# W2 by whole rows, and batch 0's second product in two rounds of twelve row blocks

## The chip, the cores and the metric

The kernel runs on one core of a Trainium2 chip. The metric is the device time of one execution in microseconds (us). The engines are TensorE (PE in the profile; its weight loads are PEld), VectorE (DVE), ScalarE (ACT), GpSimd (POOL) and SyncE (SP). SP only issues DMAs here; POOL computes and issues DMAs.

## The reference

Attention with normalised queries and keys, then a layer norm and a two-layer MLP with a residual; B, H, S, D = 8, 12, 448, 64, model width 768, hidden width 3072, all in float32:

```
q_n, k_n = rmsnorm(q, g_q), rmsnorm(k, g_k)
attn = softmax(q_n @ k_n.T / 8)            # per batch and head
x  = heads of (attn @ v) side by side      # (8, 448, 768)
xn = (x - mean) / sqrt(var + 1e-6) * g_ln
out = x + relu(xn @ w_ch1) @ w_ch2         # w_ch1 768x3072, w_ch2 3072x768
```

## The kernel before

Matmuls take float16 and sum in float32 in PSUM. A batch's 448 tokens are three tiles of 128 (t = 0, 1, 2) and 64 left over; the left tokens of two batches make one more tile. Heads go in pairs, 48 in all. For each pair seven steps of scores (L405, L411) are followed by the exponential on ACT (L421) and the product with the values (L458, L460), whose sums oA and oB DVE divides and moves into x and xl (`evac_o`, L473 to L480). There is one bank pair for oA and oB, so PE's next product with the values waits for that evacuation.

The order of the work on every engine is the order in which the program is written out. `run_rest` (L976) writes batch b's MLP chunk by chunk and after each chunk as many steps of batch b+1's attention as a quota allows; the quota is such that attention has reached its goal eleven chunks before the end of batch 0's MLP (`TAIL`). From there `run_rest` writes one item of batch 1's layer norm after each chunk (statistics, normalised rows xn, their transposes by SP's DMA, the root), and from the tenth last chunk on one weight sum after each (L763: sums and differences of blocks of W2, which later batches use in their second product).

Batch 0's MLP is `first_mlp`. `up` (L713) makes the hidden layer h, 24 blocks of 128. `down` (L723) is the second product: for each column half g of W2 (384 columns) and each token tile t, 24 matmuls, one for each block of 128 rows of W2, are summed in one PSUM bank; a chunk is six of them (s counts threes of row blocks, a chunk is two values of s). After the last row block, `add` (L754, DVE) multiplies the sum by the token's scale and adds it to x. The banks psC of these sums and psH of the hidden layer come from one pool of three banks (`ps_m`, tag "mlp"), used in rotation: a new sum takes the bank of the third last and waits for what reads that one. Stores of finished tiles are noted in `late` and issued on SP's queue by `store_late` at s = 3 of the next tile; SP's queue also holds the loads of q and k and the transposes (L306 to L318, L688).

W2 lies in on-chip memory as 24 row blocks of 768 columns in float16, and is loaded by `load_w2` on POOL's queue, with conversion from float32. Its first call comes at step 47 of attention and its second at step 71 (`W2_AT`); the second is preceded by a small copy (L613) that makes POOL wait for a DMA transpose of keys. The first call takes the left 384 columns of all 24 row blocks in one DMA, the second the right 384 columns in two DMAs of twelve row blocks.

The chunks of `down` before:

```
for g in range(2):
    for t in range(3):
        for s in range(4):   # a chunk: s = 2s, 2s + 1
```

Of the kernel before, what the change touches and what calls it, by code (L numbers as in the profile page):

```python
# [8 lines left out]
FP32 = mybir.dt.float32  # L9
# [7 lines left out]
ts = bass.ts  # L17
# [3 lines left out]
NDC, NFF = DM // 128, FF // 128  # L21
# [44 lines left out]
HALF, HCOL = NFF // 2, DM // 2  # L66
# [25 lines left out]
class _Fast:  # L92
# [518 lines left out]
    def load_w2(self, g):  # L611
        if g:
            self.nc.gpsimd.tensor_copy(out=self.rr[:, DMA_UNIT:DMA_UNIT + 1],  # L613
                                       in_=self.kU[DMA_UNIT % 2][:, 0:1])
        for c in (slice(0, HALF), slice(HALF, NFF)) if g else (slice(0, NFF),):
            self.nc.gpsimd.dma_start(
                out=self.sh.w2[:, c, ts(g, 384)],
                in_=self.w2[128 * c.start:128 * c.stop, ts(g, 384)].rearrange("(c p) d -> p c d", p=128))

    def tok_tiles(self, b):  # L620
        x = self.xs[b]
# [86 lines left out]
    def first_mlp(self):  # L708

        nc, sh = self.nc, self.sh  # L710
        tiles, xnT, hT, cur = self.tok_tiles(0), self.xnT, self.hS, {}

        def up(f, i):  # L713
            if i == 0:
                cur["h"] = self.ps_m.tile([128, 512], FP32, tag="mlp", name="psH")
            ps = cur["h"]
            for dc in range(3 * i, 3 * i + 3):
                nc.tensor.matmul(ps[:, 0:384], sh.w1[:, dc, ts(f, 128)], xnT[:, dc],
                                 start=(dc == 0), stop=(dc == NDC - 1))
            if i:  # L720
                nc.scalar.activation(out=hT[:, f], in_=ps[:, 0:384], func=AFT.Relu)

        def down(t, g, s):  # L723
            if s == 0:
                cur["ps"] = self.ps_m.tile([128, 512], FP32, tag="mlp", name="psC")
            ps = cur["ps"][:, 0:HCOL]
            for f in range(3 * s, 3 * s + 3):
                nc.tensor.matmul(ps, hT[:, f, ts(t, 128)], sh.w2[:, f, ts(g, HCOL)],
                                 start=(f == 0), stop=(f == NFF - 1))
            if s == 7:  # L730
                self.add(0, t, g, ps)
                if g and t < 2:
                    self.late.append((0, t, slice(0, DM)))
                elif t == 2 and not g:
                    self.late.append((0, t, slice(0, HCOL)))
                elif t == 2:
                    self.store(0, t, slice(HCOL, DM))
            elif s == 3:
                self.store_late()

        for f in range(UP_FIRST, NFF):
            yield 6 * 384 / 2.4, [lambda f=f, i=i: up(f, i) for i in range(2)]
        for g in range(2):
            for t in range(3):
                for s in range(4):
                    yield 6 * HCOL / 2.4, [lambda t=t, g=g, s=s: down(t, g, s)
                                           for s in (2 * s, 2 * s + 1)]

    def store_late(self):
        for a in self.late:  # L750
# [500 lines left out]
```

## Time and profile before

| what | value |
|---|---|
| median of 3 runs | 582.73 us (582.29, 582.73, 582.96) |
| profiled execution | 579.58 us |
| its span | 578.0 us |
| PE busy | 559.5 us (97%) |
| DVE busy | 381.7 us (66%) |
| ACT busy | 364.4 us (63%) |
| POOL busy | 207.0 us (36%) |
| batch 0's second product on PE | 88.3 to 118.4 us |

Start times are microseconds from the start of the span. A row of the timeline has the start, the duration, the engine, the line, the operation with its output and inputs, the shapes and the count; consecutive like instructions are merged, and what the engine waited for stands in brackets. A duration runs to the end of the write, so the next instruction of an engine can start a little before it. PE's matmuls overlap, so the time of many is read from the start of the first to the start of what follows. "w" in a row stands for W1 and W2 both, "w2s" for the memory of the weight sums, "hS" for the hidden layer.

### The profile page before, as it was taken

What the parts mean: (1) busy time and instruction counts of PE and PEld (TensorE: products, weight loads), DVE (VectorE), ACT (ScalarE), POOL (GpSimd) and SP (SyncE); (2) the same over time, 40 slices, a digit from 0 to 9 for tenths busy, and PEclk for the clock granted to TensorE, in tenths of its full rate; (3) what the DMA queues carried; (4) which work ended last, traced back from release to release, by engine and by line L of the source; (5) the groups of instructions that cost most, each with busy time, mean ns of one, the idle gap of its engine ahead of it and who ended that gap; (6) DMA issues with size and microseconds to landing.
All of it is one profiled execution on the core that took longest, in us unless ns stands there. A gap on an engine that the chain in (4) does not pass through costs nothing.

```text
span 578.0 us, 13670 instructions
## 1 busy us (share of the span) xinstructions
PE 559.5 (97%) x5446; PEld 411.9 (71%) x5446; DVE 381.7 (66%) x826; ACT 364.4 (63%) x674; POOL 207.0 (36%) x224
## 2 busy tenths in 40 slices
PE   5788999999999999999999999999999999999997
PEld 4556666687686867777677768777777777878684
DVE  6989567699657586845667586854756743664424
ACT  5998787447675779557775588637777477323130
POOL 5885636404440620654241521644242320020000
PEclk9999999999999999999999999999999999999999
DMA  8999999958672876969663798958743390030201
GB/s 206 251 238 222 214 207 165 193 147 137 124 131 77 158 127 145 127 148 121 121 106 48 184 134 136 128 143 122 145 64 65 119 113 1 1 110 1 83 2 58
DMA packets 178329, 72.59 MB, mean 126 GB/s; under 512 B 138212, under 2 KB 173220, under 8 KB 178260
## 3 DMA queue, kind: packets, MB, share of 16 engines
q1 hardware_dynamic: 133876, 52.52, 44.1%
q0 software_dynamic: 43440, 18.52, 25.2%
q8 instruction: 44, 0.72, 0.5%
q10 hardware_dynamic: 944, 0.62, 0.4%
q14 instruction: 25, 0.20, 0.1%
HBM read 52.76 MB, written 11.01 MB: 110 GB/s over the span
## 4 chain that ended last, share of the span: by engine, by line
PE 77%; DVE 1%; issue 0%; DVEq 0%
PE psH L798 33%; PE psP L821 30%; PE psS L405 7%; PE oA L458 4%; PE oB L460 1%; PE psS L411 1%; DVE qn L83 0%; DVE w2s L763 0%; DVE ssq L265 0%; DVE w L763 0%; DVE xn L662 0%; DVE hS L804 0%; DVE x L475 0%; DVE xl L757 0%; DVE xl L480 0%
## 5 line engine op out<-in xcount | busy, mean ns | idle before, releaser
L421 ACT ACTIVATE E<-psS,rr_all 128x448 f16<-128x448 f32 x336 | 204.6, 634 | 47.3 <-PE psS L405 40.3
L798 PE MATMUL psH<-xnT,w 128*128 128x256 f16 (+1 forms) x2016 | 225.7, 261 | 0.0
L798 PEld LDWEIGHTS <-w 128*128 128x128 f16 x2016 | 172.8, 98 | 24.3 <-issue 4.9
L801 ACT ACTIVATE hS<-psH 128x512 f16<-128x512 f32 x150 | 89.8, 599 | 97.2 <-PE psH L798 93.0
L821 PEld LDWEIGHTS <-hS 128*128 128x128 f16 x1080 | 100.0, 98 | 57.3 <-issue 1.1
L821 PE MATMUL psP<-w,hS 128*128 128x384 f16 x672 | 127.0, 326 | 0.0
L405 PE MATMUL psS<-qU,kU 128*128 128x448 f16 x288 | 100.9, 352 | 5.0 <-ACT E L421 3.2
L458 PEld LDWEIGHTS <-E 128*128 128x128 f16 x1008 | 70.3, 98 | 35.8 <-issue 2.8
L279 POOL TENSOR_TENSOR k<-k,gprod 128x896 f32<-128x896 f32 x18 | 38.9, 2160 | 139.5 <-ACT khl L259 113.2
L804 DVE TENSOR_TENSOR hS<-hS 128x512 f16<-128x512 f16 (+1 forms) x119 | 60.2, 512 | 19.3 <-ACT hS L801 17.8
L821 PE MATMUL psP<-w2s,hS 128*128 128x384 f16 (+1 forms) x408 | 69.9, 321 | 0.0
L458 PE MATMUL oA<-v,E 128*128 128x65 f16 x864 | 66.9, 193 | 1.1 <-ACT E L421 0.6
L757 DVE SCALAR_TENSOR_TENSOR x<-psP,rs_all,x 128x384 f32<-128x384 f32 x60 | 36.4, 617 | 42.4 <-PE psP L821 41.8
L460 PE MATMUL oB<-v,E 128*128 128x65 f16 x288 | 52.0, 193 | 0.1
L832 POOL TENSOR_TENSOR x<-x,hS 128x384 f32<-128x384 f32 x21 | 23.4, 1126 | 76.1 <-ACT hS L900 75.5
L473 DVE RECIPROCAL rec_all<-oA 128x6 f32<-128x6 f32 x48 | 9.2, 193 | 53.6 <-PE oA L458 53.5
L216 POOL DMA_DIRECT2D v<-in_v_dram x54 | 41.5, 781 | 4.0 <-PE oB L460 2.7
L405 PEld LDWEIGHTS <-kU 128*128 128x128 f16 x288 | 28.0, 98 | 11.1 <-issue 2.2
L900 ACT ACTIVATE hS<-hS,rs_all 128x384 f32<-128x384 f32 x27 | 14.6, 604 | 33.0 <-DVE hS L804 33.0
L460 PEld LDWEIGHTS <-E 128*128 128x128 f16 x336 | 32.4, 96 | 0.4 <-DVE xl L480 0.3
L83 DVE SCALAR_TENSOR_TENSOR qn<-q,rr_all 128x256 f16<-128x256 f32 (+2 forms) x69 | 24.8, 420 | 7.2 <-ACT rr_all L269 7.1
L265 DVE TENSOR_REDUCE ssq<-khl 128x14 f32<-128x896 f32 (+1 forms) x24 | 25.5, 1061 | 5.0 <-ACT khl L259 4.8
(145 smaller groups left out, 616.6 us busy)
## 6 DMA issues: line engine op xcount, KB each, us to landing
k<-in_k_dram SPq DMA_DIRECT2D x19, 384.0 KB, 4.2
q<-in_q_dram SPq DMA_DIRECT2D x18, 384.0 KB, 3.9
out_dram<-x SPq DMA_DIRECT2D x14, 384.0 KB, 3.0
w<-in_moe_w_ch_dram POOLq DMA_DIRECT2D x3, 1536.0 KB, 14.3
v<-in_v_dram POOLq DMA_DIRECT2D x54, 64.0 KB, 4.4
out_dram<-x POOLq DMA_DIRECT2D x9, 384.0 KB, 2.7
w<-in_moe_w_ch_dram POOLq DMA_DIRECT2D x1, 2304.0 KB, 22.5
w<-in_moe_w_ch_dram POOLq DMA_DIRECT2D x2, 1152.0 KB, 14.4
```

The costliest lines, as they stand in the source:

```text
L216: nc.gpsimd.dma_start(out[:, :, j, 0:D], main[:, :, j])
L265: nc.vector.tensor_reduce(out=c["ssq"][:, n], in_=c["sq", n], axis=AX.X, op=ALU.add)
L279: (nc.vector if u in DVE_KG else nc.gpsimd).tensor_tensor(out=c["t"][1], in0=c["t"][1], in1=sh.gprod.unsqueeze(1).broadcast_to([128, g, D] ...
L405: nc.tensor.matmul(ps[0][:, 0:S], c["main"][:, ts(i, 128)], c["q"][:, ts(h, S)], start=True, stop=True)
L421: nc.scalar.activation(out=o, in_=x[:, 0:S], func=AFT.Exp, scale=self.units[u][3][:, g:g + 1], bias=EXP_BIAS)
L458: nc.tensor.matmul(oA[:, t, cs], E[:, ts(t, 128)], rhs, start=(i == 0 and t == 0), stop=(i == 6 and t == 2))
L460: nc.tensor.matmul(oB[:, cs], E[:, 320:448], rhs, start=(i == 0), stop=(i == 6))
L757: self.nc.vector.scalar_tensor_tensor(out=x, in0=ps, scalar=self.rs[:, b, t:t + 1], in1=x, op0=ALU.mult, op1=ALU.add)
L798: nc.tensor.matmul(ps[:, i], sh.w1[:, dc, ts(f + i, 128)], self.xnT[:, dc, 256 - N:256], start=(i == 0 and dc == 0), stop=(i == k - 1 and ...
L801: nc.scalar.activation(out=hT[:, f:f + k], in_=ps, func=AFT.Relu)
L804: nc.vector.tensor_tensor(out=out, in0=a, in1=c, op=op)
L821: nc.tensor.matmul(bank[x][:, c], a[:, f], w[:, f, c], start=(start and f == 0), stop=(stop and f == HALF - 1))
```

## The change

`load_w2` loads whole rows of 768 columns: the first call row blocks 0 to 5 and 6 to 11, the second 12 to 17 and 18 to 23, two DMAs each. The product is made in two rounds of twelve row blocks, each summed in a bank of its own and added to x. In the first round (row blocks 0 to 11) the six sums follow each other, two chunks each. In the second round the left half goes a quarter at a time: row blocks 12 to 17 for t = 0, 1, 2 into three banks, then 18 to 23 for t = 0, 1, 2 with an add after each; then come the three right sums, two chunks each. `store_late` is called at s = 5 in place of s = 3. Nothing else is changed; the number of chunks and of matmuls is the same.

```
-        for c in (slice(0, HALF), slice(HALF, NFF)) if g else (slice(0, NFF),):
+        for c in (0, 6) if not g else (12, 18):
             self.nc.gpsimd.dma_start(
-                out=self.sh.w2[:, c, ts(g, 384)],
-                in_=self.w2[128 * c.start:128 * c.stop, ts(g, 384)].rearrange("(c p) d -> p c d", p=128))
+                out=self.sh.w2[:, c:c + 6],
+                in_=self.w2[128 * c:128 * c + 768].rearrange("(c p) d -> p c d", p=128))
...
         def down(t, g, s):
-            if s == 0:
-                cur["ps"] = self.ps_m.tile([128, 512], FP32, tag="mlp", name="psC")
-            ps = cur["ps"][:, 0:HCOL]
+            if s in (0, 4):
+                cur[t] = self.ps_m.tile([128, 512], FP32, tag="mlp", name="psC")
+            ps = cur[t][:, 0:HCOL]
             for f in range(3 * s, 3 * s + 3):
                 nc.tensor.matmul(ps, hT[:, f, ts(t, 128)], sh.w2[:, f, ts(g, HCOL)],
-                                 start=(f == 0), stop=(f == NFF - 1))
+                                 start=(f % HALF == 0), stop=(f % HALF == HALF - 1))
+            if s in (3, 7):
+                self.add(0, t, g, ps)
             if s == 7:
-                self.add(0, t, g, ps)
                 if g and t < 2:
                     self.late.append((0, t, slice(0, DM)))
...
-            elif s == 3:
+            elif s == 5:
                 self.store_late()
...
-        for g in range(2):
-            for t in range(3):
-                for s in range(4):
-                    yield 6 * HCOL / 2.4, [lambda t=t, g=g, s=s: down(t, g, s)
-                                           for s in (2 * s, 2 * s + 1)]
+        for g, s, t in ([(g, s, t) for g in range(2) for t in range(3) for s in range(2)]
+                        + [(0, s, t) for s in (2, 3) for t in range(3)]
+                        + [(1, s, t) for t in range(3) for s in (2, 3)]):
+            yield 6 * HCOL / 2.4, [lambda t=t, g=g, s=s: down(t, g, s)
+                                   for s in (2 * s, 2 * s + 1)]
```

## The prediction

> **What bounds the kernel now.** I read the busy time by stage first, then the instructions in order of time around batch 0's second product, on TensorE (PE) and on VectorE (DVE), then the waits, the DMA landings and the SP queue.
>
> Busy time by stretch (us from the span's start; busy us of each engine with its instruction count; granted clock; DMA share; GB/s):
>
> ```profile
> core 0: us, PE busy (x) PEld busy (x) DVE busy (x) ACT busy (x) POOL busy (x), PEclk, DMA share, GB/s
> 61.00:88.30 27.30, 26.55 (x244) 17.09 (x241) 15.51 (x31) 22.42 (x47) 14.93 (x17) 1.00 1.21 198
> 88.30:107.60 19.30, 19.30 (x180) 12.06 (x178) 11.97 (x26) 14.07 (x24) 8.76 (x10) 1.00 1.26 186
> 107.60:118.40 10.80, 10.80 (x69) 6.51 (x68) 10.61 (x25) 1.82 (x5) 5.54 (x7) 1.00 1.45 187
> 118.40:140.00 21.60, 21.55 (x214) 16.93 (x213) 20.88 (x35) 14.83 (x28) 6.59 (x7) 1.00 0.66 130
> 140.00:540.00 400.00, 400.00 (x3905) 299.07 (x3904) 255.18 (x578) 254.70 (x466) 130.42 (x141) 1.00 0.63 107
> ```
>
> PE is the bound: it has 0.75 us idle from 61 to 88.3, none to 118.4, 0.05 to 140 and none to 540. So the change has at most 0.8 us to win in the stage that it touches, and whatever it makes PE wait there stays in the span, because no later PE wait can shrink. The row to look at twice is that of 107.60 to 118.40: DVE is busy for 10.61 of 10.80 us, and to 140 for 20.88 of 21.60. In these 30 us DVE runs as full as PE, though its share of the span is 66%.
>
> The second product of batch 0 has 144 matmuls, 24 chunks of 6. Their end on PE:
>
> ```profile
> L728 PE MATMUL psC<-w,hS x144: 324/326/336, 88.3 to 118.2; 128*128 128x384 f16 x144
> ...
> 105.03 1.14 PE L728 MATMUL psC<-w,hS 128*128 128x384 f16 x6
> ...
> 107.62 10.90 PE L728 MATMUL psC<-w,hS 128*128 128x384 f16 x66
> 118.36 1.47 PE L798 MATMUL psH<-xnT,w 128*128 128x256 f16 x12
> ```
>
> The reader is to see that the last 66 matmuls, chunks 14 to 24, run without any attention between them (attention has reached its goal), from 107.62 to 118.36: 0.976 us a chunk. So chunk 16 ends at 110.55 and chunk 18 at 107.62 + 5 x 0.976 = 112.50.
>
> DVE in the same stretch:
>
> ```profile
> 101.07 0.62 DVE L757 SCALAR_TENSOR_TENSOR x<-psC,rs_all,x 128x384 f32<-128x384 f32 x1
> 105.72 0.62 DVE L757 SCALAR_TENSOR_TENSOR x<-psC,rs_all,x 128x384 f32<-128x384 f32 x1 [4.04 <-PE psC L728]
> 106.62 1.09 DVE L265 TENSOR_REDUCE ssq<-khl 128x14 f32<-128x896 f32 x1 [0.28 <-ACT khl L259]
> ...
> 112.30 1.01 DVE L662 SCALAR_TENSOR_TENSOR xn<-x,stat,gln 128x768 f16<-128x768 f32 x1
> 113.35 0.62 DVE L757 SCALAR_TENSOR_TENSOR x<-psC,rs_all,x 128x384 f32<-128x384 f32 x1
> 113.88 0.75 DVE L763 TENSOR_TENSOR w2s<-w,w2s 128x1152 f16<-128x1152 f16 x1
> ...
> 116.68 0.61 DVE L757 SCALAR_TENSOR_TENSOR x<-psC,rs_all,x 128x384 f32<-128x384 f32 x1
> ...
> 119.34 0.61 DVE L757 SCALAR_TENSOR_TENSOR x<-psC,rs_all,x 128x384 f32<-128x384 f32 x1
> 119.86 0.75 DVE L763 TENSOR_TENSOR w<-w 128x1152 f16<-128x1152 f16 x1
> ```
>
> The six adds of L757 follow chunks 4, 8, 12, 16, 20 and 24. That of chunk 12 waits 4.04 us for PE: until then DVE has time. From 106.62 it has none: statistics and the normalised rows of batch 1, weight sums and adds run end to end, and the add of chunk 16, whose matmuls end at 110.55, starts at 113.35 and is done at 113.97. DVE is about 2.8 us behind PE. Today nobody minds, because the bank that it frees is wanted a whole bank rotation later.
>
> **The change, part by part.** *The load of W2.* The same bytes go in four pieces of 1152 KB instead of one of 2304 and two of 1152; runs are twice as long.
>
> ```profile
> L607 POOL DMA_DIRECT2D w<-in_moe_w_ch_dram x3: 821/883/892, 23.6 to 38.4; - x3
> L616 POOL DMA_DIRECT2D w<-in_moe_w_ch_dram x3: 1032/1063/1507, 61.4 to 88.6; - x3
> DMA to landing us min/median/max: 10.9/17.8/22.5
> 61.42 1.51 POOL L616 DMA_DIRECT2D w<-in_moe_w_ch_dram  x1
> 87.57 2.09 POOL L616 DMA_DIRECT2D w<-in_moe_w_ch_dram  x2
> ```
>
> POOL's issue at 61.42 takes 1.51 us; two pieces take between 2 x 0.82 (the W1 rows, long runs) and 2 x 1.03, so POOL's queue is 0.1 to 0.6 us later. I take 0.1, since a piece now has the W1 loads' 128 x 6 runs. The pair at 87.57 gives 0 to 0.4 us back. What covers this is the PE row of 61 to 88.3, which waits for no POOL work; were that cover gone, 0.6 us would show. The first load lands at 61.4 + 22.5 = 83.9, before the first chunk at 88.3, and holds what the first round needs. The second pair lands at about 98.5 and 88.6 + 17.8 = 106.4. Its first piece is first read by chunk 13 (105.5), its last by chunk 16 (109.6); before, by chunk 15 (108.6). Nobody waited before, nobody need wait after: 0 us both ways. Splitting the left part into quarters buys 1 us of slack that was not missing.
>
> *Six more adds.* Every sum is now added in two halves. Adds follow chunks 2, 4, 6, 8, 10, 12, then (t = 0, 1, 2 in quarters) 16, 17, 18, then 20, 22, 24. New ones are 2, 6, 10, 17, 18, 22. From one add to the next instruction DVE takes 113.88 - 113.35 = 0.53 us. In the first round the adds of chunks 2 and 6 stand before an evacuation of attention's sums, for which PE's next use of the bank waits:
>
> ```profile
> 92.72 0.30 DVE L480 TENSOR_TENSOR xl<-oB,rec_all 64x128 f32<-64x128 f32 x1
> 100.74 0.29 DVE L480 TENSOR_TENSOR xl<-oB,rec_all 64x128 f32<-64x128 f32 x1
> 94.45 0.26 PE L458 MATMUL oA<-v,E 128*128 128x65 f16 x3
> 101.90 0.25 PE L458 MATMUL oA<-v,E 128*128 128x65 f16 x3
> ```
>
> The evacuations end at 93.02 and 101.03; PE comes back at 94.45 and 101.90. Slacks of 1.4 and 0.9 us hold one add of 0.53 each. The add of chunk 10 falls into the 4.04 us of waiting. First round: 0 us (bounds 0 and 3 x 0.53 = 1.6 if every one reached PE; I take 0, as the slacks are larger than the add).
>
> *The banks.* psH and psC share three banks in rotation. Chunks 13, 14, 15 now open all three (t = 0, 1, 2 of the left half), and chunk 19, the first of the right half, needs the bank of chunk 16's sum. PE is there at 112.50. DVE's list from 105.72 to the add of chunk 16 is unchanged (the new adds of the second round come behind it), so that add still ends at 113.97. PE waits 113.97 - 112.50 = 1.47 us. Chunks 21 and 23 need the adds of 17 and 18: each stands behind one weight sum of 0.75, so they end by 113.88 + 0.75 + 0.62 = 115.3 and by about 116.6, while PE is there at 115.9 and 117.9: no wait. So **1.47 us** of PE waiting, at one place. What queues behind the waiting chunk on PE is everything.
>
> *DVE's list up to 131 us.* Behind chunk 16 DVE has three more adds, 17, 18 and 22: 3 x 0.53 = 1.59 us, and its list stays without a gap up to here:
>
> ```profile
> 129.90 0.19 DVE L473 RECIPROCAL rec_all<-oA 128x6 f32<-128x6 f32 x1
> 130.92 0.29 DVE L480 TENSOR_TENSOR xl<-oB,rec_all 64x128 f32<-64x128 f32 x1
> 128.25 0.22 PE L460 MATMUL oB<-vl,E 128*128 128x130 f16 x1
> 131.27 0.20 PE L460 MATMUL oB<-v,E 128*128 128x65 f16 x1
> PEld L460 <- DVE xl L480: 0.2, 1, 0.2
> ```
>
> PE finished that sum at 128.47; DVE takes it up at 129.90, and PE's next oB at 131.27 has waited 0.2 us for it. DVE has no slack there, so its 1.59 us arrive at PE. They don't add to the 1.47: PE, already 1.47 later, waits 0.12 more. Total **1.59 us**.
>
> *The SP queue.* The left store of t = 2 moves from chunk 14 to 19, that of t = 0 from 18 to 21, of t = 1 from 22 to 23.
>
> ```profile
> 115.27 4.17 SPq L312 DMA_TRANSPOSE qU<-qn  x3
> 119.54 1.00 SPq L956 DMA_DIRECT2D out_dram<-x  x2
> 120.59 3.09 SPq L318 DMA_TRANSPOSE qU<-qn  x2
> 129.62 0.35 PE L405 MATMUL psS<-qU,kU 128*128 128x448 f16 x1
> ```
>
> The three transposes at 115.27 move ahead of two stores (0 to 0.6 us earlier). The two at 120.59 stand behind the last store, whose add now ends at about 121.3 instead of 119.95, so they issue about 1.3 us later, done by 125 plus the landing; PE reads them at 129.62, itself 1.5 us later. 0 us.
>
> *PE's own work* is the same 144 matmuls. New semaphore waits (two pieces, six banks) may take 51 ns each:
>
> ```profile
> L728 PEldq EVENT_SEMAPHORE  x7: 51/51/51, 86.7 to 97.9; - x7
> ```
>
> Seven such lie in the stage where PE idles 0.00 us, so I take 0; at most 8 x 0.05 = 0.4.
>
> **Sum.** 0 (loads) + 0 (first round) + 1.47 (bank) + 0.12 (DVE at 131) + 0 = +1.6 us. The profiled execution took 579.58 us (span 578.0, 1.6 around it), so 581.2 against it. The median of the runs, 582.73, is 3.15 above that execution; carried over, **584.3 us**, 0.27% slower. The form of the cost: one TensorE wait near 112.5, and a span longer from there on.
>
> **The rivals.** *Not slower: lighter transfers let DVE run ahead.* The DMA share is 1.21 and 1.26 from 61 to 107.6, more than full. If longer runs lighten it, preparation (and DVE's list) could come earlier. It decides if DVE ends the add of chunk 16 before 112.50, 1.47 us earlier. For it: the only gap behind 105.72 is a wait of 0.28 for the scalar engine. Against: the list starts behind an add that waits for PE at 105.72, and no transfer moves that. Price: no wait, and up to the 0.75 us that PE idles between 61 and 88.3: 582.0 to 582.7. Chance 0.14, of which 0.05 faster by over 0.2%.
>
> *The W2 pieces come late.* The third and fourth land after chunks 13 and 16 want them. They'd have to slip by 7 and by 3.2 us, and the fourth by 3.2 + 1.5 before it costs more than the forecast, since a PE wait at chunk 16 takes the place of the bank wait. Even the longest landing of the rows, 22.5 us, puts it at 88.6 + 22.5 = 111.1, 1.5 late: 584.3 again. At 25 us it lands at 113.6, 4.0 late: 586.8. Against: longer runs and an earlier end of POOL's issue. Chance 0.05.
>
> *The first round pays too.* DVE's adds in the first round reach PE at the evacuations: up to 1.6 us more, 585.9. Against: slacks of 1.4 and 0.9. Chance 0.08.
>
> *The clock falls.*
>
> ```profile
> PE psW L532 <- POOL id masks.py:199: 2.7, 1, 2.7
> 0.00:15.00 15.00, 8.55 (x79) 6.72 (x80) 10.22 (x22) 8.08 (x18) 8.02 (x14) 1.00 0.82 210
> ```
>
> The first 15 us hold a PE wait of 2.7 us and 6.45 us of idle at a granted clock of 1.00; by these rows a wait of 1.5 us costs only itself. If PE ran at half clock for as long as it waited and some 2 us more, the sum would rise by about 1.7: 586.0. Chance 0.03. [...]
>
> **How the numbers follow.** The forecast has 0.70, with a range of its own of 583.8 to 584.9 (the add done 0.3 us earlier or semaphores at 0.4). Runs of a kernel spread by 0.3 to 0.4 us, so 0.2% (1.17 us; the line is at 583.9) is about what can be told from no change. The forecast lies 0.4 above that line: of its 0.70, 0.60 is slower and 0.10 within. With the rivals: faster 0.05; within 0.09 + 0.10 = 0.19; slower 0.60 + 0.05 + 0.08 + 0.03 = 0.76. The range takes in half of the first rival and most of the late pieces and first round: 582.6 to 585.8.
>
> **What the changed profile would show.** Right: after chunk 18 (t = 2, left, last quarter) PE waits about 1.5 us for a DVE add of L757; DVE has no gap from about 106 to 132; PE's first product of batch 1 starts at about 119.9 instead of 118.36; six psC adds more, each 0.62; nothing of W2 waited for. Wrong, if chunk 19 follows without a gap, if DVE's add of chunk 16 ends by 112.5, if PE waits for a transfer, or if PE idles again before 540 for a cause that isn't there now.

## The result and the profile after

The changed kernel takes 583.28 us (median of 21 runs, 581.55 to 584.59) beside 582.02 us before (21 runs, 580.18 to 584.96): a ratio of 1.002, with a 95% interval of 1.001 to 1.0029. It is slower, by about 1.3 us between the medians.

The profiled executions differ by more: spans of 578.0 and 581.4 us. The last additions of DVE and the spans tell why (timeline, before and after):

```profile
574.20 0.42 DVE L757 SCALAR_TENSOR_TENSOR xl<-psP,rs_all,xl 128x192 f32<-128x192 f32 x1 [0.57 <-PE psP L821]
```

```profile
575.90 0.42 DVE L758 SCALAR_TENSOR_TENSOR xl<-psP,rs_all,xl 128x192 f32<-128x192 f32 x1 [0.57 <-PE psP L822]
```

That addition is 1.7 us later after the change; the other 1.7 us lie behind it (578.0 - 574.2 = 3.8 and 581.4 - 575.9 = 5.5 us for the same last stores). From the start of PE's last matmul to the end of the span it is 4.1 us in the profile of before and 5.6 to 5.9 us in all nine others of this study, so the execution of before that was profiled had an uncommonly short end. Places inside the span are compared below, not spans.

Busy time by stretch after the change (columns as in the prediction):

```profile
core 0: us, PE busy (x) PEld busy (x) DVE busy (x) ACT busy (x) POOL busy (x), PEclk, DMA share, GB/s
88.30:107.60 19.30, 19.30 (x181) 12.19 (x179) 13.33 (x29) 13.95 (x24) 7.20 (x8) 1.00 1.27 204
107.60:118.40 10.80, 9.45 (x60) 5.49 (x57) 10.64 (x26) 2.03 (x5) 5.76 (x7) 1.00 0.77 100
118.40:142.00 23.60, 23.60 (x229) 18.43 (x227) 22.88 (x39) 15.02 (x28) 6.82 (x7) 1.00 0.73 144
142.00:543.00 401.00, 401.00 (x3909) 299.46 (x3907) 255.50 (x578) 254.45 (x465) 130.10 (x140) 1.00 0.63 107
```

PE has lost 1.35 of 10.80 us from 107.6 to 118.4; from 88.3 to 543 the profile counts no other idle time of PE. PE's rows there, and the product with the values behind the evacuation (timeline):

```profile
107.83 5.05 PE L728 MATMUL psC<-w,hS 128*128 128x384 f16 x30
114.23 6.01 PE L728 MATMUL psC<-w,hS 128*128 128x384 f16 x36 [1.35 <-DVE x L758]
120.08 1.47 PE L799 MATMUL psH<-xnT,w 128*128 128x256 f16 x12
...
132.69 0.25 PE L458 MATMUL oA<-v,E 128*128 128x65 f16 x3
132.81 0.20 PE L460 MATMUL oB<-v,E 128*128 128x65 f16 x1
```

The 66 matmuls that ran without a gap are now 30, a wait, and 36. Thirty matmuls are five chunks: the wait stands before chunk 19, and an add of DVE ends it. DVE in the same time:

```profile
105.93 0.62 DVE L758 SCALAR_TENSOR_TENSOR x<-psC,rs_all,x 128x384 f32<-128x384 f32 x1 [2.26 <-PE psC L728]
...
113.56 0.62 DVE L758 SCALAR_TENSOR_TENSOR x<-psC,rs_all,x 128x384 f32<-128x384 f32 x1
114.09 0.75 DVE L764 TENSOR_TENSOR w2s<-w,w2s 128x1152 f16<-128x1152 f16 x1
114.76 0.61 DVE L758 SCALAR_TENSOR_TENSOR x<-psC,rs_all,x 128x384 f32<-128x384 f32 x1
115.29 0.75 DVE L764 TENSOR_TENSOR w2s<-w 128x1152 f16<-128x1152 f16 x1
115.95 0.61 DVE L758 SCALAR_TENSOR_TENSOR x<-psC,rs_all,x 128x384 f32<-128x384 f32 x1
116.48 0.75 DVE L764 TENSOR_TENSOR w2s<-w,w2s 128x1152 f16<-128x1152 f16 x1
...
120.87 0.61 DVE L758 SCALAR_TENSOR_TENSOR x<-psC,rs_all,x 128x384 f32<-128x384 f32 x1
...
132.46 0.29 DVE L480 TENSOR_TENSOR xl<-oB,rec_all 64x128 f32<-64x128 f32 x1
```

The add of chunk 16 stands where it stood (113.56 beside 113.35; this whole execution was already 0.21 us later at the product's first matmul), adds 17 and 18 follow it, and the evacuation ends at 132.75 instead of 131.21. PE's next oB starts at 132.81, as soon as that is done.

The loads of W2 after the change (one line's instructions, then POOL's timeline):

```profile
L616 POOL DMA_DIRECT2D w<-in_moe_w_ch_dram x4: 826/855/917, 61.6 to 86.4; - x4
DMA to landing us min/median/max: 11.0/13.8/18.2
```

```profile
61.64 1.75 POOL L616 DMA_DIRECT2D w<-in_moe_w_ch_dram  x2
...
85.28 0.18 POOL L613 CAST rr_all<-kU 128x1 f32<-128x1 f16 x1 [5.76 <-DMA kU<-khl]
85.51 1.70 POOL L616 DMA_DIRECT2D w<-in_moe_w_ch_dram  x2
```

The pieces land no later than 86.4 + 18.2 = 104.6 us, and the last is wanted at 109.8. PE waits for none of them.

### The profile page after: what moved, and what is told of

Read it like the earlier page. It is cut to its first block, busy times and chain, and to the rows that moved or that the text cites. A ratio compares the mean times of both kernels' runs of the same rounds, so it can differ in the third digit from the quotient of the medians.

```text
span 581.4 us, 13673 instructions
## 1 busy us (share of the span) xinstructions
PE 559.7 (96%) x5446; PEld 412.0 (71%) x5446; DVE 385.3 (66%) x832; ACT 364.5 (63%) x674; POOL 206.8 (36%) x225
## 4 chain that ended last, share of the span: by engine, by line
PE 84%; DVE 7%; ACT 3%; issue 2%; DMA 2%; SPq 0%; POOL 0%; ACTq 0%; DVEq 0%; POOLq 0%
PE psH L799 34%; PE psP L822 30%; PE psS L405 8%; PE oA L458 5%; PE psH L718 2%; ACT E L421 2%; DVE ssq L265 2%; PE oB L460 2%; PE psS L411 1%; DMA q<-in_q_dram 1%; PE psC L728 1%; DVE stat L641 1%; ACT khl L259 1%; DVE qn L83 1%; DMA w2s<-in_k_dram 1%
## 5 line engine op out<-in xcount | busy, mean ns | idle before, releaser
L405 PE MATMUL psS<-qU,kU 128*128 128x448 f16 x288 | 100.9, 352 | 5.0 <-ACT E L421 3.2
L405 PEld LDWEIGHTS <-kU 128*128 128x128 f16 x288 | 28.0, 98 | 11.1 <-issue 2.2
```

The source lines that it names most:

```text
L405: nc.tensor.matmul(ps[0][:, 0:S], c["main"][:, ts(i, 128)], c["q"][:, ts(h, S)], start=True, stop=True)
```

## The experiments

The theory: DVE's list from 106 to 131 us is full, and PE meets it at two places, at the bank of chunk 16's sum and at the evacuation near 131; whichever of the two is later sets the loss. The rivals: the bank alone costs the time, by its order in quarters; the loads cost or gain something; six adds cost by their number, wherever they stand.

The times hardly tell the kernels apart, since the runs of one kernel scatter by some us. The traces tell more. The table gives, for the same matmul in PE's order (the four columns are the matmul's place in the kernel before), how much later it starts than in the kernel before, less the same difference at the first matmul of batch 0's second product (0.1 to 0.5 us, from the span's first 18 us). Each row is one execution. The ratio of times is beside it, from 10 to 21 runs of the kernel (one alone of rows, one round) and 21 to 35 of the one before, taken along with them.

| kernel | 112.5 us (chunk 19) | 118.5 us (batch 1) | 140 us | last matmul | ratio to before (95%) |
|---|---|---|---|---|---|
| changed | 1.51 | 1.51 | 1.32 | 1.49 | 1.002 (1.001 to 1.0029) |
| fourth bank | 0.00 | 0.00 | 1.33 | 2.04 | 1.0009 (0.9995 to 1.0022) |
| pairs | 0.00 | 0.15 | 1.40 | 1.49 | 1.0014 (1.0002 to 1.0026) |
| early sums | 0.84 | 0.84 | 0.62 | 0.87 | 1.0008 (0.9997 to 1.002) |
| bank and early sums | 0.00 | 0.00 | -0.22 | 0.09 | 0.9998 (0.9988 to 1.0008) |
| three sums in the list | 0.00 | 0.00 | 2.25 | 2.50 | 1.0028 (1.0012 to 1.0045) |
| three sums in the gap | 0.00 | 0.00 | 0.01 | 0.47 | 0.9993 (0.9973 to 1.0013) |
| rows, one round | 10.09 | 10.09 | 10.09 | 10.19 | one run, 591.52 us |
| rounds, halves | 1.62 | 1.61 | 1.44 | 1.72 | 1.0034 (1.0019 to 1.0049) |

What is added between 140 us and the last matmul (0.1 to 0.7 us, 0.46 even where the edit had done nothing up to 140) comes in one or two steps, near 219 and 352 us of the kernel before, where a product of scores (L405) starts up to 0.5 us later. The size differs from execution to execution; what sets it is not shown. So the column to compare is that of 140 us.

**A fourth bank.** Only chunk 19's sum moves, to a bank of the scores' pool:

```
-                cur[t] = self.ps_m.tile([128, 512], FP32, tag="mlp", name="psC")
+                cur[t] = (self.ps_s.tile([128, 512], FP32, tag="psS", name="psC") if (t, g, s) == (0, 1, 4)
+                          else self.ps_m.tile([128, 512], FP32, tag="mlp", name="psC"))
```

> The changed kernel, but the first right sum of the second round (chunk 19) goes into a bank of the scores' pool, which is idle there; nothing else differs, and DVE's list is the same. Theory (DVE's list up to 131 us is full, so three adds more arrive at PE whether or not a bank is waited for): the 1.35 us wait before chunk 19 is gone, batch 1's first product starts at about 118.6 instead of 120.1, but PE then waits about 1.4 us for the evacuation near 131, and the end is the changed kernel's: 1.2 to 1.5 us above before. Rival (only the bank cost time): no wait at either place, time within 0.3 us of before.

PE in this run (timeline), and PE's weight loads' waits from 107 to 134 us:

```profile
107.95 10.90 PE L729 MATMUL psC<-w,hS 128*128 128x384 f16 x66
118.69 1.47 PE L800 MATMUL psH<-xnT,w 128*128 128x256 f16 x12
...
132.61 0.27 PE L458 MATMUL oA<-v,E 128*128 128x65 f16 x3 [0.74 <-DVE x L475]
```

```profile
PEld L458 <- DVE x L475: 1.2, 1, 1.2
```

The wait before chunk 19 is gone, all 66 matmuls run on end again, and batch 1 starts at 118.69. But at 132.61 PE waits for DVE, and by 140 us it is as late as in the changed kernel (1.33 and 1.32). The bank wait cost nothing that the evacuation would not have cost; the rival that only the bank matters falls by the trace. The measured time (0.09% above before, interval -0.05 to 0.22%) is lower than the 1.2 us I expected, and its interval holds the expected 1.2 us as well as the rival's 0.3.

**Pairs.** The left part of the second round tile by tile:

```
-                        + [(0, s, t) for s in (2, 3) for t in range(3)]
+                        + [(0, s, t) for t in range(3) for s in (2, 3)]
```

> The changed kernel, but the left part of the second round is summed tile by tile (two chunks each) and not a quarter at a time, so no bank is wanted before it is free; the six added sums stay. Theory (DVE's list): no wait before chunk 19, but a wait of about 1.4 us at the evacuation near 131; 1.2 to 1.5 us above before. Rival (the quarters' bank order costs it): within 0.3 us of before. W2's last piece lands at about 102, before its new need at 108.6, so no wait for W2 by either.

The longest wait of PE and that of its weight loads from 88 to 145 us, both at the evacuation:

```profile
PE oA L458 <- DVE x L475: 0.7, 1, 0.7
```

```profile
PEld L458 <- DVE x L475: 1.1, 1, 1.1
```

No wait before chunk 19, none for W2, and 1.40 us at 140: about the same as with quarters. One thing I had not expected: chunk 21 starts 0.15 us late, at 115.14, because it takes the bank of chunk 16's sum, whose add ends at 115.09. The order in quarters costs nothing by itself and buys nothing; what costs is the adds, as long as DVE's list is full.

**Early sums.** In the changed kernel the first twelve row blocks are there from 81 us on, so four of the weight sums can be made in DVE's waiting:

```
                 ops, last = self.weight_sums()
+                ops = ops[0::2] + ops[1::2]
...
-                if (left < 10 if b == 0 else b == 1) and ops:
-                    ops.pop(0)()
+                for _ in range(({15: 1, 14: 1, 13: 2, 7: 1, 6: 1, 5: 1, 4: 1}.get(left, 0) if b == 0 else b == 1)):
+                    if ops:
+                        ops.pop(0)()
```

> The changed kernel with four of the eight weight sums of batch 0 (those that need only the first twelve row blocks) moved ahead into DVE's waiting at chunks 9 to 11, the other four behind chunks 17 to 20: DVE's list behind 106 us is 4 x 0.67 = 2.7 us shorter, and 0.67 of it before the add of chunk 16. Theory: the wait before chunk 19 shrinks from 1.35 to about 0.7, the wait at 131 is gone; 0.5 to 0.7 us above before. Rival (the wait does not come from DVE's backlog): 1.2 us above before, as the changed kernel.

```profile
108.09 5.05 PE L728 MATMUL psC<-w,hS 128*128 128x384 f16 x30
113.82 6.01 PE L728 MATMUL psC<-w,hS 128*128 128x384 f16 x36 [0.68 <-DVE x L758]
```

One weight sum less ahead of chunk 16's add takes 0.67 us from the wait (1.35 to 0.68). Behind it the list is short enough that the evacuation is in time; even the kernel before's own wait there (0.2 us) goes, and 0.62 us are left at 140. Here the bank is what costs.

**Bank and early sums.** Both edits in one.

> Both: chunk 19's sum in a bank of the scores' pool, and four weight sums moved ahead. Theory: no PE wait between 88 and 140, before's 0.2 us at 131 gone too; 0 to 0.2 us below before. Rival (the loads of W2, or six adds as such, cost something that is neither the bank nor the list): stays 0.5 us or more above before.

```profile
108.05 10.90 PE L729 MATMUL psC<-w,hS 128*128 128x384 f16 x66
118.78 1.47 PE L800 MATMUL psH<-xnT,w 128*128 128x256 f16 x12
```

No wait from 88 to 140 us, and 0.22 us ahead of before at 140. With the two waits gone the six adds, the whole rows and the quarters cost nothing that could be seen: the whole loss up to 140 us is explained. Set side by side, the bank alone is worth 0.62 + 0.22 = 0.84 us where the list is short, and 1.32 - 1.33, nothing, where it is full. The time is that of before (0.9998, interval 0.9988 to 1.0008): a lead of 0.04% is not one that these runs can tell, and no version here beats both by measurement.

**Three sums in the list, three in the gap.** Two kernels made from the one before. The first repeats one weight sum three times behind the first chunk of batch 1, the second another one behind chunk 11, in DVE's wait of 4 us; they give the same values again.

```
                 ops, last = self.weight_sums()
+                again = [ops[6]]
...
+                if b == 1 and again:
+                    for _ in range(3):
+                        again[-1]()
+                    again = []
```

```
+                if b == 0 and left == 13:
+                    for _ in range(3):
+                        ops[0]()
```

> The kernel before, with one weight sum of DVE (0.67 us from start to start) done three times more behind batch 1's first chunk of matmuls, that is after every add of batch 0 and ahead of the evacuation near 131; it gives the same values again. Theory (DVE's list has no slack up to there): PE waits about 2.0 us more at the evacuation and the end is 2.0 us later, 0.35%. Rival (DVE has slack, only banks cost): within 0.3 us of before.

> The same three extra weight sums, but behind chunk 11 of the kernel before, in DVE's wait of 4.0 us for chunk 12. Theory: within 0.2 us of before, since DVE waits there for PE anyway. Rival (any DVE work more costs its time): 2.0 us later.

The waits of PE and of ACT from 110 to 140 us with the sums in the list (what waited, for what, us in total, times, longest):

```profile
PE psH L798 <- ACT hS L801: 1.2, 1, 1.2
PE oA L458 <- DVE x L475: 0.7, 1, 0.7
```

```profile
ACT rt L268 <- DVE ssq L265: 3.9, 1, 3.9
```

And DVE with the sums in the gap:

```profile
101.73 2.33 DVE L763 TENSOR_TENSOR w2s<-w 128x1152 f16<-128x1152 f16 x3
105.85 0.62 DVE L757 SCALAR_TENSOR_TENSOR x<-psC,rs_all,x 128x384 f32<-128x384 f32 x1 [1.78 <-PE psC L728]
```

In the list, 2.25 us of DVE work become 2.25 us of PE time, with no bank of batch 0 in play. I had expected 2.0, by 0.67 us for each sum, but a repeat that writes the same place as the sum just before it started 0.78 to 0.79 us behind it. In the gap the same work shortens a wait from 4.0 to 1.8 us and moves PE by 0.01. The list has no slack, the gap has. The list reaches PE by a second way that I had not named: ACT's root L268 waits 3.9 us for a DVE sum (1.6 us in the kernel before), the activations of the hidden layer queue behind it, and PE waits for their bank.

**Rows, one round.** The kernel before with the new `load_w2` alone.

> The kernel before with W2 loaded by whole rows alone, the product in one round as before. Row blocks 12 to 17 are then wanted at 92 us and 18 to 23 at 94, and in the changed kernel they land at about 96.5 and 102. Theory (loads and rounds belong together; the loads alone gain nothing): PE waits 4 us and 4 us more for W2, 8 to 9 us later than before. Rival (whole rows are so much quicker that they help by themselves): less than 2 us later, or faster.

PE in this run (timeline), and busy time by stretch (the last three numbers are the granted clock, the DMA share and GB/s):

```profile
96.10 2.08 PE L728 MATMUL psC<-w,hS 128*128 128x384 f16 x6 [3.65 <-DMA w<-in_moe_w_ch_dram]
101.81 2.08 PE L728 MATMUL psC<-w,hS 128*128 128x384 f16 x6 [3.26 <-DMA w<-in_moe_w_ch_dram]
```

```profile
92.00:96.00 4.00, 0.44 (x4) 0.11 (x3) 2.35 (x7) 1.67 (x3) 3.93 (x5) 0.92 1.18 203
96.00:97.50 1.50, 1.40 (x5) 0.69 (x5) 0.00 (x0) 0.00 (x0) 1.50 (x3) 0.50 1.17 210
103.50:105.50 2.00, 2.00 (x15) 1.08 (x14) 1.57 (x5) 0.64 (x1) 0.00 (x0) 0.50 0.01 4
105.50:108.00 2.50, 2.50 (x26) 1.62 (x25) 2.38 (x7) 1.61 (x4) 0.00 (x0) 0.98 0.01 2
```

PE waits 3.65 and 3.26 us for the third and fourth piece. The rest of the 10.1 us is the clock: after the first wait the granted clock is 0.50 until about 105.5, and six matmuls take 2.08 us instead of 1.14. I had expected 8 to 9 us, by the waits alone. The loads by rows need the product in rounds.

**Rounds, halves.** The changed kernel with the old `load_w2`.

> The changed kernel with W2 loaded by column halves as before. The right half's first piece is then wanted at about 97.8 us (chunk 7) and lands at about 98.5. Theory (the loads by rows gain nothing but this): PE waits 0.5 to 1.0 us at chunk 7, the wait before chunk 19 stays near 1.4; 0.5 to 1.0 us above the changed kernel, 1.7 to 2.3 above before. Rival (loading by rows costs time elsewhere): below the changed kernel.

```profile
98.20 1.14 PE L728 MATMUL psC<-w,hS 128*128 128x384 f16 x6
...
114.64 6.01 PE L728 MATMUL psC<-w,hS 128*128 128x384 f16 x36 [1.35 <-DVE x L758]
```

The expected wait at chunk 7 is not there: from chunk 6 to 105 us PE's difference grows by 0.10 us, not by 0.5 to 1.0. The piece landed at 87.2 + 10.9 = 98.1 us, 0.4 earlier than I had put it, and chunk 7 starts at 98.2, so the margin is narrow. The wait before chunk 19 is again 1.35 us, and 1.44 us are left at 140, beside 1.32. So by these two executions the loads by rows are worth about 0.1 us to this product, and cost none; the two intervals of time (1.0019 to 1.0049 and 1.001 to 1.0029) overlap.

## Why the prediction was right, and where its terms were off

- *PE is the bound, and what it waits in this stage stays in the span.* Right: PE is busy for all of 142 to 543 us after the change, and the last addition is 1.7 us later, the 0.2 from the span's start among it.
- *The loads cost 0.* Right. POOL's first issue went from 1.51 to 1.75 us, inside the 0.1 to 0.6 given. The second pair was issued 2 us earlier (85.51 instead of 87.57), because the transpose that POOL waits for was done earlier; nobody waited for that either.
- *The first round costs 0.* Right: PE's difference is 0.00 at 97.5 and 105 us; no add reached PE. The first evacuation ended 0.53 us later, by one whole add, within its slack of 1.4. The second ended only 0.04 us later, and not because of the 0.9 us of slack: in the kernel before DVE had waited 0.70 us for PE just ahead of that evacuation (at 99.72), and the add took the place of that wait. The prediction had not counted it.
- *The bank, 1.47 us before chunk 19.* Right in place, engine and cause; measured 1.35 as a wait, 1.51 as a shift of the matmul. The early sums showed that it is DVE's place in its list that makes it: 0.67 less list, 0.67 less wait.
- *DVE's list up to 131, 1.59 us, 0.12 of them beyond the bank.* This term was mis-sized. The list was 1.53 - 0.21 = 1.32 us longer (its last add went from 119.34 to 120.87), so PE, 1.51 late by then, didn't wait for it, and before's own wait of 0.2 us went: 1.51 fell to 1.32 instead of rising to 1.59. Three adds at 0.53 should have made 1.59. Most of the missing 0.27 stands in the rows of before that I did not count:

```profile
114.55 0.75 DVE L763 TENSOR_TENSOR w2s<-w 128x1152 f16<-128x1152 f16 x1
115.33 0.76 DVE L763 TENSOR_TENSOR w2s<-w,w2s 128x1152 f16<-128x1152 f16 x1
116.01 0.75 DVE L763 TENSOR_TENSOR w2s<-w 128x1152 f16<-128x1152 f16 x1
```

The second of these reads what the first has just written, and starts 0.78 us behind it, the third 0.68 behind the second. The kernel before has two such pairs in the list (the other starts at 117.87); after the change an add stands between the two sums of each, and whatever follows a weight sum starts 0.66 to 0.67 us behind it. So 2 x 0.11 us went out of the list as the adds came in. The profiles of all ten kernels bear this out: where one weight sum directly follows another, it starts 0.78 to 0.79 us behind it in the 8 cases where it reads what that one wrote and in the 4 where it writes the same place again, and 0.66 to 0.68 us in the 28 others. The remaining 0.05 us are not explained.

- *The SP queue and PE's own work, 0.* Right: PE was busy for all 23.60 us from 118.4 to 142, so it waited for no transpose, and the new semaphores show nowhere.
- *The sum, 1.6 us, and 584.3.* The trace gives 1.3 at 140 us and 1.5 at the last matmul, the medians 1.26. Of the 1.0 us between 584.3 and 583.28, 0.7 come from the base (582.73 by three runs, 582.02 by 21) and 0.3 from the sum. So 583.28 lies in the range of 582.6 to 585.8, but below the forecast's own 583.8 to 584.9, and the measured 0.2% lies on the line that the prediction drew between slower and no change. The runs of a kernel also spread more than the 0.3 to 0.4 us that were read from three: by 4.8 us over 21.
- *The rivals.* DVE did not run ahead: its add of chunk 12 waited for PE as before, and the list behind it kept its times. The pieces were not late, the first round did not pay, and the clock stayed at 1.00 through the wait of 1.35 us. That wait is what settles the clock; the row of the first 15 us, by which the prediction argued, does not. Its clock column says 1.00, but 24 matmuls of L532 from 5.98 us on took 2.74 us (114 ns each), and 16 of the same shape from 15.05 us on 1.06 us (66 ns each): PE ran slower in those first microseconds than the column says, and its wait of 2.7 us, the very first, tells nothing of what a wait does to a full clock.

## What to carry to other kernels

An engine that is two thirds busy over the span can be full in the one stage that an edit touches: read its list there, instruction by instruction, and look for where the bounding engine next meets it. Work added to a full list arrives at the bound once, at the later of the meeting points and not at their sum, so taking the wait for the bank away showed nothing until the list was shorter too; the same work in a gap of the list was free. When three banks are opened at once, ask when the reader of the first will have read it, not when its sum was ready.

## What the runs showed that was not expected

- A wait of PE of 1.35 us left the granted clock at 1.00 (107.6 to 118.4 us, after), one of 3.65 us brought it to 0.50 for about 10 us, with a second wait in between (rows, one round). The Trainium skill, "TensorE: Matmul & The Clock Gate", section "What's actually happening", puts the fall to half rate at one idle window of about 3.4 us or more; these two runs agree. A third shows that such a wait is not the only way: with the three sums in the list the granted clock was 0.50 from 14.7 to 18.0 us (16 matmuls of L532 took 1.91 us there, 1.06 in the kernel before), though PE had not waited longer than 1.1 us since 4 us. What brought it is not shown.
- A sum of DVE in fp16 that reads what the sum just before it wrote, or writes the same place, started 0.78 to 0.79 us behind it, one that does neither 0.66 to 0.68 us.
- From the start of PE's last matmul to the end of the span it was 4.1 us in one profiled execution and 5.6 to 5.9 in nine: a difference larger than what the whole change costs.
